# Delta-rule attention and soft MoE on one core: products over two heads on 64-row tiles, a zero-padded state, a 32-column block inverse on VectorE

## The chip, the cores and the metric

The kernel runs on one core of a Trainium2 chip. The metric is device time in microseconds (us) for one launch. The profiled execution is one launch of its own, recorded by the hardware profiler; its time is shown beside the median of the unprofiled runs.

## What is computed

Two blocks follow each other. The first is delta-rule attention over 4 batches, 8 heads, 768 positions and head size 48; the second is a soft mixture of 8 experts with 4 slots each, on rows of 384 numbers.

```
k_n = k / (norm(k) + 1e-06)
for t in range(S):
    y[:, :, t] = q[:, :, t] @ state
    v_old      = k_n[:, :, t] @ state
    state      = state + beta[t] * outer(k_n[t], v[t] - v_old)
x = y with the heads side by side: (3072, 384)
logits = x @ phi                       # 32 slots
d = softmax(logits, over rows);  slot_input = d.T @ x
slot_out[e] = relu(slot_input[e] @ w1[e]) @ w2[e]
out = softmax(logits, over slots) @ slot_out
```

## The kernel before

**Chunks.** The recurrence is done in 24 chunks of C = 32 positions, six groups of GC = 4 chunks. The 32 pairs of batch and head are laid out as four heads `h` on the partitions (32 positions each, slices `hs`) times U = 8 pairs of batch `b` and half `g` in the free dimension. Within a chunk the recurrence becomes matrix products and the inverse of a unit lower triangular 32x32 matrix for each pair.

**Preparation (`prep`).** K and Q of a chunk are loaded by twelve DMAs with V (`loads`, L439), turned by products with the identity (L503), copied to KQ (`copy`: L325 on ScalarE, L327 on VectorE), and multiplied to the Gram matrices K·K and K·Q (L473). The first is copied to Lc, the second multiplied by a triangular mask into AT (L490).

**Inverse (`invert`, once a group).** A 32x32 block transpose puts the four chunks' matrices into lanes (L535). The norms come from the diagonal with two powers on POOL (L541, L544). VectorE inverts the two 16x16 diagonal blocks of each matrix by elimination, 15 pairs of a product and a subtraction (L587, L603), turns them back (L609, L613), POOL or ScalarE mask them (L641, L639), and two sets of products on TensorE give the block below the diagonal (N1, L653, and N2, L666; then L672). The first group does that in four parts, one a chunk; the others in one.

**Chunk loop (`chunk`).** In order: V is scaled by the norms on POOL (L691); R reads the state with K (L704) and the residual is V minus that (L715); W solves with the inverse (L727); evU copies the result; KU adds K times it to the state (L748). Two heads of the state accumulate in two PSUM banks throughout the scan, two are added on VectorE (L760), and both halves are copied to SBUF. Q reads the old state with Q (L704), AU adds AT times U (L771), and evY copies the output, which four DMAs a chunk (`rel`, L783) move to rows of X. Every fourth chunk `route` does the router for 128 positions of each batch (L799, L811, L867). At the end `experts` runs two layers (L1015, L1046) and writes 24 output tiles (L1088).

**What sets the order.** A planner written in the kernel (`Plan`) gives every operation a cost, a priority (the longest path after it, plus a bias) and the buffers it needs (SLOTS, and eight PSUM banks), and simulates the engines. Instructions are then issued to each engine in the order of the planned starts; each engine follows its own order, and waits where an operand isn't there. Expert weights use the scan's buffers as they die; SP issues most loads.

```
SLOTS = dict(K=15, Q=4, V=5, KQ=12, AT=12, Lc=2, lb=1, lbs=1, tt=2, pr=2, Dt=1, Dc=1, M1=1,
...
plan = Plan(SLOTS, 8, 2, 0.15)
...
for o in sorted(plan.ops, key=lambda o: (o.start, o.prio)):
    o.fn(o.eng)
```

Of the kernel before, what the change touches and what calls it, by code (L numbers as in the profile page):

```python
# [35 lines left out]
class Plan:  # L36
# [67 lines left out]
    def run(self, backing=()):  # L104
# [45 lines left out]
        def place(v):  # L150
# [11 lines left out]
            for i in range(0, self.banks - n + 1):  # L162
                if not any(held[i:i + n]):
                    t = max(bank[i:i + n])
                    if best is None or t < best[0]:
                        best = (t, i)
# [77 lines left out]
def kernel(  # L244
# [31 lines left out]
    SIZE = dict(K=U * D, Q=U * D, V=U * D, KQ=B * 2 * P, AT=U * C, Lc=C * C,  # L276
                lb=1056, lbs=512, tt=512, pr=512, Dt=512, Dc=512, M1=512, D0=1024, P1=512,
                TT=C * C, R=U * D, U=U * D, Y=U * D, S=4 * BD, X=B * Dm, XT=B * P,
                lT=P, dT=P, d=P, el=P, cT=P, wt=NKT * F, hr=F, hT=NFC * P, ob=Dm, sj=Dm, so=Dm,
                cw=P, sl=NKT * NSL)  # L280
    SLOTS = dict(K=15, Q=4, V=5, KQ=12, AT=12, Lc=2, lb=1, lbs=1, tt=2, pr=2, Dt=1, Dc=1, M1=1,
                 D0=1, P1=1, TT=2, R=2, U=2, Y=3, S=2, X=2, XT=3, lT=2, dT=1, d=1, el=1, cT=NG,
                 hr=1, hT=2, ob=6, sj=1, so=1, cw=2, sl=1)
    KEEP = ("cT",)
    OBP, HTP, RBIAS, EB = 0, 11, 30.0, 40.0
    TAIL = ("hr", "hT", "ob", "sj", "so", "cw", "sl")
    plan = Plan(SLOTS, 8, 2, 0.15)
    plan.limits = dict(tp=2, pg=2)
# [42 lines left out]

    def vc(n):
        return 0.06 + 0.00104 * n

    hs = [slice(C * h, C * h + C) for h in range(4)]
    rs_ = [slice(DP * g, DP * g + D) for g in range(G)]
# [6 lines left out]
    expo = const("expo", [P, 2])  # L343
# [24 lines left out]
    def constants(e):  # L368
        make_identity(nc, ident)
        PO.memset(expo[:, 0:1], 0.5)  # L370
        PO.memset(expo[:, 1:2], -2.0)
# [15 lines left out]
    op("const2", [("DVE", 1.0)], constants2, [cv], [cv])  # L387

    zv = [val("", "st") for _ in range(2)]

    def zero_banks(e):
        for i in range(8):
            nc.vector.memset(banks[:, i], 0.0)
    op("zero", [("DVE", 3.0)], zero_banks, [], [zv[0]])

    def clear_d0(e):
        for i in range(SLOTS["D0"]):
            PO.memset(where["D0", i].rearrange("p (u s) -> p u s", s=C)[:, :, HC:C], 0.0)
    d0v = val("", "st")
    op("d0", [("POOL", 0.6)], clear_d0, [], [d0v])  # L400
# [9 lines left out]
    def make_sel(e):  # L410
        PO.memset(sel, 0.0)
        for c in range(GC):
            PO.tensor_copy(
                sel[:, c].rearrange("p (h c b g) -> p c h b g", h=4, c=GC, b=B)[:, c],
                ident[0:C, 0:C].rearrange("p (b g h) -> p h b g", b=B, g=G))
# [21 lines left out]
    def load(src, x, cc, h):  # L437
        def fn(e):
            dge[e].dma_start(  # L439
                out=sb(x, U, D)[hs[h]],  # L440
# [11 lines left out]
    KQv, ATv, Lcv = {}, {}, {}  # L452

    def prep(cc):
# [5 lines left out]
        lc = Lcv[n]  # L460
        split = n == 0

        def gram(parts, x):
            def fn(e):
                t = ps(x)
                kt = sb(kq, B, 2, P)
                n0 = len(parts) * C
                for b in range(B):
                    for h in range(4):
                        for g in range(G):  # L470
                            rhs = kt[rs_[g], b, :, hs[h]] if len(parts) == 2 else \
                                kt[rs_[g], b, parts[0], hs[h]]
                            PE.matmul(t[hs[h], g, b * n0:(b + 1) * n0],  # L473
                                      lhsT=kt[rs_[g], b, 0, hs[h]], rhs=rhs,
                                      start=True, stop=True, skip_group_check=True)
            return fn

        def ev_l(x, np_):
            def fn(e):
                src = ps(x)[:, :, 0:B * np_ * C].rearrange("p g (b a t) -> p g b a t", b=B, a=np_)  # L480
                dst = sb(lc, GC, B, G, C)[:, c].rearrange("p b g t -> p g b t")
                copy(e, dst, src[:, :, :, 0, :])
            return fn

        def ev_a(x, np_):
            def fn(e):
                src = ps(x)[:, :, 0:B * np_ * C].rearrange("p g (b a t) -> p g b a t", b=B, a=np_)
                dst = sb(at, G, B, C)
                for g in range(1):
                    nc.vector.tensor_tensor(  # L490
                        dst, src[:, :, :, np_ - 1, :],
                        tri.unsqueeze(1).unsqueeze(1).broadcast_to([P, G, B, C]), op=ALU.mult)
            return fn

        for a, src, L in ((0, Kv, "K"), (1, Qv, "Q")):
# [3 lines left out]
            def tr(e, s=s, tp=tp):  # L499
                t, m = ps(tp, B, P), sb(s, B, G, D)  # L500
                for b in range(B):
                    for g in range(G):
                        PE.matmul(t[rs_[g], b, :], lhsT=m[:, b, g, :], rhs=ident, start=True,  # L503
                                  stop=True, skip_group_check=True)
            op(f"tr{L}{cc}", [("PE", 0.46)], tr, [s, cv], [tp, kq])
# [4 lines left out]
            if split:  # L510
                x = val("pg", "ps", 2)
                op(f"gram{L}{cc}", [("PE", 0.5)], gram((a,), x), [kq], [x, at if a else lc])
                if a == 0:
                    op(f"evL{cc}", [("ACT", 0.4), ("DVE", 0.42)], ev_l(x, 1), [x], [lc], bias=EB)
                else:
                    op(f"evA{cc}", [("DVE", 0.42)], ev_a(x, 1), [x, cv], [at], bias=EB)
        if not split:
            x = val("pg", "ps", 2)
            op(f"gram{cc}", [("PE", 0.58)], gram((0, 1), x), [kq], [x, lc, at])
# [661 lines left out]
```

## Time and profile before

| Figure | Before |
|---|---|
| median of three runs (range) | 518.09 us (515.16 to 520.31) |
| profiled execution, and its span | 509.47 us, 507.8 us |
| mean granted TensorE clock | 0.674 of full |
| first solve (L727) starts | 51.9 us |
| last output product (L771) ends | 444.4 us |
| HBM read and written | 39.47 MB, 4.72 MB |

How to read a profile: times are microseconds, PE is TensorE's matmuls and PEld its weight loads, DVE is VectorE, ACT ScalarE, POOL GpSimd, SP the queue that issues most DMAs. A name such as L704 is a line of the kernel. Rows of the timeline and of the windows give a start or a stretch first, then busy time and, behind an x, the number of instructions; brackets hold the idle time before a row and what ended it. In the windows the last figures are the granted clock, the DMA engines' busy share and GB/s. One call of a product in fp32 shows as two matmul records.

### The profile page before, as it was taken

The page shows a single profiled execution, that of the slowest core. Times are in us where ns is not written, and L with a number is a line of the kernel's source. Part 1 is how long each engine was busy: PE and PEld are TensorE (multiplying, and loading weights), DVE is VectorE, ACT ScalarE, POOL GpSimd, SP SyncE. Part 2 cuts the span into 40 slices and gives each one's busy share as a digit, 9 for nine tenths or more (in the row PEclk, how much of TensorE's full clock was granted, in tenths as well). Part 3 has the DMA queues.
Part 4 walks back from the last instruction along what each step waited for, and adds up shares of the span by engine and source line. Part 5 has one row for each costly group of instructions (what it writes and reads, how often), then busy time and mean ns, then how long its engine had stood idle before and what let it go on. Part 6 is the DMA issues. An engine that isn't in the chain of part 4 may idle for free.

```text
span 507.8 us, 29272 instructions
## 1 busy us (share of the span) xinstructions
PE 344.6 (68%) x13716; PEld 274.9 (54%) x13716; DVE 181.4 (36%) x465; ACT 79.4 (16%) x162; POOL 128.1 (25%) x119
## 2 busy tenths in 40 slices
PE   6737575666776755778567876676755567859974
PEld 5636574555665644666556655455644456533432
DVE  5436225502242512344333453334341122442232
ACT  1114001120121401022300222000220000110022
POOL 4364720050810305400618003180050000000022
PEclk9987559565586955597755885555675555767995
DMA  6643024344014430144111420326534455189837
GB/s 126 122 85 62 5 50 80 59 73 78 4 36 78 74 66 4 30 78 76 21 19 20 70 51 17 102 65 165 158 85 168 137 156 178 20 281 404 327 123 251
DMA packets 115209, 50.81 MB, mean 100 GB/s; under 512 B 105760, under 2 KB 107296, under 8 KB 115088
## 3 DMA queue, kind: packets, MB, share of 16 engines
q1 hardware_dynamic: 89536, 42.05, 32.5%
q10 hardware_dynamic: 24752, 4.48, 5.0%
q8 instruction: 108, 1.77, 1.5%
q0 software_dynamic: 800, 2.41, 1.3%
q14 instruction: 13, 0.11, 0.1%
HBM read 39.47 MB, written 4.72 MB: 87 GB/s over the span
## 4 chain that ended last, share of the span: by engine, by line
PE 50%; issue 32%; DMA 6%; DVE 4%; POOL 3%; SPq 3%; ACT 1%; ACTq 1%; POOLq 0%; DVEq 0%
PE banks L704 8%; PE banks L503 7%; PE banks L771 7%; PE banks L727 6%; PE banks L666 5%; PE banks L748 5%; PE banks L653 5%; PE banks L473 4%; SPq L439 3%; DMA arena<-in_q_dram 2%; PE banks L799 2%; DMA arena<-in_k_dram 1%; DMA arena<-arena 1%; PE banks L867 1%; POOL nrall L541 1%
## 5 line engine op out<-in xcount | busy, mean ns | idle before, releaser
L325 ACT ACTIVATE arena<-banks 128x384 f32<-128x384 f32 (+3 forms) x109 | 55.0, 507 | 372.2 <-PE banks L748 121.4
L327 DVE COPY arena<-banks 128x512 f32<-128x512 f32 (+3 forms) x77 | 43.2, 561 | 133.1 <-PE banks L503 38.5
L503 PE MATMUL banks<-ident,arena 128*48 128x128 f32 x768 | 63.7, 325 | 14.2 <-DMA arena<-in_k_dram 6.1
L704 PE MATMUL banks<-arena 48*32 48x48 f32 x2944 | 48.3, 254 | 30.0 <-issue 29.2
L503 PEld LDWEIGHTS banks<-ident,arena 128*48 128x48 f32 x768 | 53.3, 149 | 20.8 <-issue 13.4
L641 POOL TENSOR_SCALAR arena<-arena,half 128x512 f32<-128x512 f32 (+1 forms) x12 | 19.0, 1597 | 166.5 <-DVE arena L609 78.8
L704 PEld LDWEIGHTS banks<-arena 48*32 48x32 f32 x2944 | 37.9, 130 | 40.7 <-issue 35.3
L771 PE MATMUL banks<-arena 32*32 32x48 f32 x1536 | 35.5, 256 | 16.2 <-issue 16.2
L727 PE MATMUL banks<-arena 32*32 32x48 f32 x1536 | 33.3, 246 | 18.0 <-issue 11.7
L473 PE MATMUL banks<-arena 48*32 48x64 f32 (+1 forms) x1792 | 29.5, 249 | 17.1 <-issue 8.9
L771 PEld LDWEIGHTS banks<-arena 32*32 32x32 f32 x1536 | 29.5, 145 | 20.7 <-issue 19.0
L727 PEld LDWEIGHTS banks<-arena 32*32 32x32 f32 x1536 | 28.1, 138 | 22.5 <-issue 14.5
L653 PE MATMUL banks<-arena 32*32 32x16 f32 x1536 | 24.8, 206 | 19.3 <-issue 18.7
L1088 POOL DMA_DIRECT2D out_dram<-arena x12 | 6.6, 551 | 118.8 <-DVE arena L1084 118.8
L748 PE MATMUL banks<-arena 32*48 32x48 f32 x1472 | 26.4, 266 | 14.1 <-issue 14.1
L666 PE MATMUL banks<-arena 32*32 32x16 f32 x1536 | 26.3, 210 | 13.7 <-issue 13.5
L473 PEld LDWEIGHTS banks<-arena 48*32 48x32 f32 x1792 | 22.8, 122 | 22.5 <-issue 19.9
L653 PEld LDWEIGHTS banks<-arena 32*32 32x32 f32 x1536 | 22.4, 144 | 22.2 <-issue 20.2
L541 POOL TENSOR_TENSOR nrall<-nrall,expo 128x32 f32<-128x32 f32 x6 | 32.7, 5446 | 0.5
L544 POOL TENSOR_TENSOR gmall<-nrall,expo 128x32 f32<-128x32 f32 x6 | 32.7, 5444 | 0.5
L666 PEld LDWEIGHTS banks<-arena 32*32 32x32 f32 x1536 | 24.0, 150 | 16.0 <-issue 15.7
L748 PEld LDWEIGHTS banks<-arena 32*48 32x48 f32 x1472 | 21.4, 160 | 20.0 <-issue 19.0
(110 smaller groups left out, 330.1 us busy)
## 6 DMA issues: line engine op xcount, KB each, us to landing
arena<-in_moe_w_dram SPq DMA_DIRECT2D x24, 512.0 KB, 5.1
arena<-in_moe_w_dram SPq DMA_DIRECT2D x32, 384.0 KB, 7.7
arena<-in_q_dram SPq DMA_DIRECT2D x88, 48.0 KB, 2.5
arena<-in_k_dram SPq DMA_DIRECT2D x87, 48.0 KB, 2.9
arena<-in_v_dram SPq DMA_DIRECT2D x80, 48.0 KB, 2.6
arena<-arena ACTq DMA_DIRECT2D x58, 48.0 KB, 2.3
out_dram<-arena SPq DMA_DIRECT2D x12, 192.0 KB, 2.7
out_dram<-arena POOLq DMA_DIRECT2D x12, 192.0 KB, 3.0
```

Source lines behind the costliest of these rows:

```text
L325: AC.activation(dst, src, ACT.Copy)
L327: nc.vector.tensor_copy(dst, src)
L473: PE.matmul(t[hs[h], g, b * n0:(b + 1) * n0], lhsT=kt[rs_[g], b, 0, hs[h]], rhs=rhs, start=True, stop=True, skip_group_check=True)
L503: PE.matmul(t[rs_[g], b, :], lhsT=m[:, b, g, :], rhs=ident, start=True, stop=True, skip_group_check=True)
L541: PO.tensor_tensor(nrall[:, n], nrall[:, n], expo[:, 0:1].broadcast_to([P, C]), op=ALU.pow)
L544: PO.tensor_tensor(gmall[:, n], nrall[:, n], expo[:, 1:2].broadcast_to([P, C]), op=ALU.pow)
L653: PE.matmul(t[hs[h], u], lhsT=sb(lc, C, C)[hs[h], u], rhs=sb(M1, C, HC)[hs[h], u], start=True, stop=True, skip_group_check=True)
L666: PE.matmul(t[hs[h], u], lhsT=sb(D0, C, C)[hs[h], u], rhs=sb(P1, C, HC)[hs[h], u], start=True, stop=True, skip_group_check=True)
L704: PE.matmul(t[hs[h], g, b * D:(b + 1) * D], lhsT=m[rs_[g], b, a, hs[h]], rhs=s[rs_[g], h, b], start=(b == 0), stop=False, skip_group_check ...
L727: PE.matmul(t[hs[h], u], lhsT=m[hs[h], u], rhs=r[hs[h], u], start=(u == 0), stop=True, skip_group_check=True)
L748: PE.matmul(dst[rs_[g], b * D:(b + 1) * D], lhsT=m[hs[h], b * G + g], rhs=r[hs[h], b * G + g], start=(b == 0 and (h >= 2 or cc == 0)), sto ...
L771: PE.matmul(t[hs[h], g, b * D:(b + 1) * D], lhsT=m[hs[h], g, b], rhs=r[hs[h], b * G + g], start=(cc == 0 and b == 0), stop=True, skip_grou ...
```

## The change

Products in the scan take two heads at a time, or all rows. K and Q lie in SBUF padded from 48 to 64 numbers, so that one transpose turns both halves `g` of a batch. The state keeps `g` as two row blocks of 64 with a zero block beside each (its buffers are cleared once), so that R and Q read it with all 128 rows and 96 columns, and KU writes 128 rows into four PSUM banks that are held through the scan. The Gram product takes two heads on a 64x64 tile; its off-diagonal blocks are masked out, for K·K by two scaled copies on ScalarE and a sum (evL, evM, adL), for K·Q by a copy and a mask on POOL (evA, mkA). The inverse is spread into pairs with zero blocks (`pairs`, TP), for W on 64-row tiles; AU uses the same tiles. `par` and `tri2` are the masks of even and odd heads.

For groups two to six the inverse is an elimination over all 32 columns on VectorE, 31 pairs of steps, without N1 and N2. The norms come from an integer estimate and three Newton steps in place of the powers. Slot counts, biases and the planner's costs of products change too; a product's cost is now at least four times 12.5 ns a call in the plan.

```diff
...
+    SLOTS = dict(K=11, Q=4, V=5, KQ=10, AT=10, Lc=2, Lx=2, lb=2, tt=2, pr=2, Dt=1, Dc=1,
+                 M1=1, D0=1, P1=1, TP=8, R=2, U=2, Y=3, S=2, X=2, XT=3, lT=2, dT=1, d=1, el=1,
+                 cT=NG, hr=1, hT=2, ob=6, sj=1, so=1, cw=2, sl=1)
...
+    OBP, HTP, RBIAS, EB, IBIAS, FETCH = 0, 11, 40.0, 60.0, -5.0, 0.0125
-    plan = Plan(SLOTS, 8, 2, 0.15)
-    plan.limits = dict(tp=2, pg=2)
+    plan = Plan(SLOTS, 8, 0, 0.15)
+    plan.limits = dict(tp=2, pg=2, py=2)
...
+    def pe(mm, array):
+        return [("PE", max(array, FETCH * 4 * mm))]
...
-    rs_ = [slice(DP * g, DP * g + D) for g in range(G)]
+    hp_ = [slice(2 * C * i, 2 * C * i + 2 * C) for i in range(2)]
+    rs_ = [slice(DP * g, DP * g + DP) for g in range(G)]
...
+    for i in range(SLOTS["K"]):
+        for t in ("K", "Q"):
+            if i < SLOTS[t]:
+                padv[t, i] = val("", "st")
+                op(f"pad{t}{i}", [("POOL", 0.3), ("DVE", 0.2)],
+                   lambda e, t=t, i=i: clear(e, where[t, i].rearrange(
+                       "p (u d) -> p u d", d=DP)[:, :, D:DP]), [], [padv[t, i]],
+                   bias=50 - i if i < 4 else 0)
...
+            pad = sb(x).shape[1] // U
             dge[e].dma_start(
-                out=sb(x, U, D)[hs[h]],
+                out=sb(x, U, pad)[hs[h], :, 0:D],
...
+                kt = sb(kq, B, 2, 4, C)
+                m = len(parts) * 2 * C
                 for b in range(B):
-                    for h in range(4):
+                    for hp in range(2):
                         for g in range(G):
...
-                            PE.matmul(t[hs[h], g, b * n0:(b + 1) * n0],
-                                      lhsT=kt[rs_[g], b, 0, hs[h]], rhs=rhs,
-                                      start=True, stop=True, skip_group_check=True)
+                            h2 = slice(2 * hp, 2 * hp + 2)
+                            rhs = kt[rs_[g], b, :, h2].rearrange("p a h t -> p h a t")
...
+                            PE.matmul(t[hp_[hp], g, b * m:(b + 1) * m],
+                                      lhsT=kt[rs_[g], b, 0, h2].rearrange("p h t -> p (h t)"),
+                                      rhs=rhs, start=True, stop=True, skip_group_check=True)
...
-        def ev_l(x, np_):
...
+        def ev_l(x, np_, i, dst):
             def fn(e):
...
+                AC.activation(dst(), view(x, np_, 0)[:, :, :, i], ACT.Copy, scale=par[:, i:i + 1])
             return fn
         def ev_a(x, np_):
             def fn(e):
...
-                    nc.vector.tensor_tensor(
-                        dst, src[:, :, :, np_ - 1, :],
-                        tri.unsqueeze(1).unsqueeze(1).broadcast_to([P, G, B, C]), op=ALU.mult)
+                for g in range(G):
+                    copy(e, sb(at, G, B, 2, C)[:, g], view(x, np_, np_ - 1)[:, g])
             return fn
+        def evs_l(x, np_):
+            dst = lambda: sb(lc, GC, G, B, C)[:, c]
+            op(f"evL{cc}", [("ACT", 0.4)], ev_l(x, np_, 0, dst), [x, cv], [lc, lcp[cc]], bias=EB)
+            op(f"evM{cc}", [("ACT", 0.4)], ev_l(x, np_, 1, lambda: sb(lx, G, B, C)), [x, cv], [lx],
+               bias=EB)
...
+        def evs_a(x, np_):
+            op(f"evA{cc}", pcost2(512), ev_a(x, np_), [x], [at], bias=EB)
+            def mask(e):
+                v_ = nc.vector if e == "DVE" else PO
+                t = sb(at, U, 2, C)
+                v_.tensor_tensor(t, t, tri2.unsqueeze(1).broadcast_to([P, U, 2, C]), op=ALU.mult)
+            op(f"mkA{cc}", [("POOL", 1.15)], mask, [at, cv], [at])
...
-                t, m = ps(tp, B, P), sb(s, B, G, D)
+                t, m = ps(tp, B, P), sb(s, B, G * DP)
                 for b in range(B):
-                    for g in range(G):
-                        PE.matmul(t[rs_[g], b, :], lhsT=m[:, b, g, :], rhs=ident, start=True,
-                                  stop=True, skip_group_check=True)
-            op(f"tr{L}{cc}", [("PE", 0.46)], tr, [s, cv], [tp, kq])
+                    PE.transpose(t[:, b, :], m[:, b, :], ident)
...
+    def pairs(n, c, src, reads, uses):
+        x = TPv[GC * n + c] = val("TP", par=True)
+        for i in range(2):
+            def fn(e, i=i):
+                dst = sb(x, U, 2, C)[:, :, i]
+                if e == "ACT":
+                    AC.activation(dst, src(), ACT.Copy, scale=par[:, i:i + 1])
+                else:
+                    PO.tensor_scalar(dst, src(), par[:, i:i + 1], None, op0=ALU.mult)
+            op(f"TP{GC * n + c}", [("ACT", 0.42), ("POOL", 0.9)], fn, reads + [cv], [x], uses=uses)
...
-        def norms(e):
-            PO.tensor_tensor(nrall[:, n], nrall[:, n], expo[:, 0:1].broadcast_to([P, C]),
-                             op=ALU.pow)
-            PO.tensor_tensor(gmall[:, n], nrall[:, n], expo[:, 1:2].broadcast_to([P, C]),
-                             op=ALU.pow)
-        op(f"norms{n}", [("POOL", 2.0)], norms, [lb, bbv, cv], [gv])
...
+        def newton(e):
+            v_ = nc.vector if e == "DVE" else PO
+            for _ in range(3):
+                v_.tensor_tensor(gm, nr, dg(), op=ALU.mult)
+                v_.tensor_tensor(gm, gm, nr, op=ALU.mult)
+                v_.tensor_scalar(gm, gm, -0.5, 1.5, op0=ALU.mult, op1=ALU.add)
+                v_.tensor_tensor(nr, nr, gm, op=ALU.mult)
+            v_.tensor_tensor(nr, nr, dg(), op=ALU.mult)
+            v_.tensor_scalar(nr, nr, 1e-6, None, op0=ALU.add)
+        op(f"nw{n}", [(E0, 2.6 if n == 0 else 4.5)], newton, [lb, s1], [s1])
...
+        if n:
+            lm = lambda: sb(lb)[:, 0:C * C].rearrange("p (i j) -> p i j", j=C)
...
+            for j in range(C - 1):
+                m, w = j + 1, C - 1 - j
+                pr = val("pr")
+                def e1(e, j=j, m=m, w=w, pr=pr):
+                    t, s, o = sb(tt, C, C), lm(), sb(pr)[:, 0:w * m]
...
+                        nc.vector.tensor_tensor(
+                            o.rearrange("p (i k) -> p i k", i=w),
+                            t[:, j, 0:m].unsqueeze(1).broadcast_to([P, w, m]),
+                            s[:, j + 1:C, j].unsqueeze(2).broadcast_to([P, w, m]), op=ALU.mult)
+                op(f"el{n}.{j}a", [("DVE", vc(w * m))], e1, [tt, lb], [pr])
+                def e2(e, j=j, m=m, w=w, pr=pr):
+                    t, o = sb(tt, C, C), sb(pr)[:, 0:w * m]
+                    d = t[:, 1:C, 0] if m == 1 else t[:, j + 1:C, 0:m]
...
+                    nc.vector.tensor_tensor(d, d, o, op=ALU.subtract)
+                op(f"el{n}.{j}b", [("DVE", vc(w * m))], e2, [tt, pr], [tt])
...
+            return
...
-    keep = val("keep", "st")
+    keep = val("keep", "ps", 4)
...
-        py = val("py", "ps", 2)
+        py = val("py", "ps")
         def read(a, x):
             def fn(e):
-                t, m, s = ps(x), sb(kq, B, 2, P), sb(old, 4, B, D)
+                t, m, s = ps(x, B, G * D), sb(kq, B, 2, P), sb(old, 4, B, G * D)
                 for b in range(B):
                     for h in range(4):
-                        for g in range(G):
-                            PE.matmul(t[hs[h], g, b * D:(b + 1) * D], lhsT=m[rs_[g], b, a, hs[h]],
-                                      rhs=s[rs_[g], h, b], start=(b == 0), stop=False,
-                                      skip_group_check=True)
+                        PE.matmul(t[hs[h], b], lhsT=m[:, b, a, hs[h]], rhs=s[:, h, b],
+                                  start=(b == 0), stop=False, skip_group_check=True)
             return fn
         if cc:
             R = val("R", par=True)
...
         def solve(e):
-            t, m = ps(pw, U, D), sb(T, C, C)[:, c * U:c * U + U]
-            r = sb(R, U, D) if cc else sb(vv, U, D)
-            for u in range(U):
-                for h in range(4):
-                    PE.matmul(t[hs[h], u], lhsT=m[hs[h], u], rhs=r[hs[h], u],
-                              start=(u == 0), stop=True, skip_group_check=True)
-        wo = op(f"W{cc}", [("PE", 0.7)], solve, [TTp[n][c], R] if cc else [TTp[n][c], vv, vs], [pw, Uv],
-           uses=[T])
+            t, m, r = ps(pw, B, G, D), sb(TP, G, B, 2 * C), sb(R if cc else vv, B, G, D)
+            for b in range(B):
+                for g in range(G):
+                    for i in range(2):
+                        PE.matmul(t[hp_[i], b, g], lhsT=m[hp_[i], g, b], rhs=r[hp_[i], b, g],
+                                  start=(b == 0 and g == 0), stop=True, skip_group_check=True)
+        wo = op(f"W{cc}", pe(16, 0.68), solve, [TP, R] if cc else [TP, vv, vs], [pw, Uv])
...
         if cc < NCH - 1:
             new = Sv[cc + 1] = val("S", par=True)
-            ks = val("ks", "ps", 2)
             def update(e):
-                m, r, t = sb(kk, U, D), sb(Uv, U, D), ps(ks)
+                m, r = sb(kk, B, P), sb(Uv, B, G * D)
                 for b in range(B):
-                    for g in range(G):
-                        for h in range(4):
-                            dst = banks[:, h] if h < 2 else t[:, h - 2]
-                            PE.matmul(dst[rs_[g], b * D:(b + 1) * D],
-                                      lhsT=m[hs[h], b * G + g], rhs=r[hs[h], b * G + g],
-                                      start=(b == 0 and (h >= 2 or cc == 0)), stop=True,
-                                      skip_group_check=True)
-            op(f"KU{cc}", [("PE", 0.62)], update, [kk, Uv, zv[0]], [ks, keep])
...
+                    for h in range(4):
+                        PE.matmul(banks[:, h, b * G * D:(b + 1) * G * D], lhsT=m[hs[h], b],
+                                  rhs=r[hs[h], b], start=(cc == 0 and b == 0), stop=True,
+                                  skip_group_check=True)
+            op(f"KU{cc}", pe(16, 0.66), update, [kk, Uv], [keep])
+            for g in range(G):
+                def ev_s(e, g=g):
+                    copy(e, sb(new, 4, B, G, D)[rs_[g], :, :, g],
+                         banks[rs_[g], 0:4, 0:B * G * D].rearrange("p h (b g d) -> p h b g d", b=B,
+                                                                  g=G)[:, :, :, g])
+                op(f"evS{cc}", pcost(768), ev_s, [keep] + s0v, [new], bias=EB)
...
```

## The prediction

> **What bounds the kernel now.** I first read the page's busy shares, then its chain of waits, then its DMA queues, then the timeline of TensorE in the middle, then its windows.
>
> ```profile
> span 507.8 us, 29272 instructions
> PE 344.6 (68%) x13716; PEld 274.9 (54%) x13716; DVE 181.4 (36%) x465; ACT 79.4 (16%) x162; POOL 128.1 (25%) x119
> ...
> q8 instruction: 108, 1.77, 1.5%
> ...
> PE 50%; issue 32%; DMA 6%; DVE 4%; POOL 3%; SPq 3%; ACT 1%; ACTq 1%; POOLq 0%; DVEq 0%
> ```
>
> The chain is TensorE (50%) plus "issue" (32%, 160 us), time in which TensorE waits for nobody. 39 us of it is the expert stage's pipelined matmuls; some 120 us lie in the scan. The timeline, TensorE only, shows what they are:
>
> ```profile
> 200.28 1.47 PE L666 MATMUL banks<-arena 32*32 32x16 f32 x94
> 203.36 0.71 PE L666 MATMUL banks<-arena 32*32 32x16 f32 x34 [1.61 <-issue]
> 204.00 1.37 PE L704 MATMUL banks<-arena 48*32 48x48 f32 x93
> 207.47 0.69 PE L704 MATMUL banks<-arena 48*32 48x48 f32 x35 [2.10 <-issue]
> 208.09 1.50 PE L771 MATMUL banks<-arena 32*32 32x48 f32 x64
> 209.37 0.84 PE L727 MATMUL banks<-arena 32*32 32x48 f32 x29
> 211.20 1.01 PE L727 MATMUL banks<-arena 32*32 32x48 f32 x35 [0.98 <-issue]
> ```
>
> From stop to stop are 34+93 and 35+64+29 matmul records: 128, with their weight loads 256 instructions, wherever a product ends. The page's instruction queue moved 108 packets of 1.77 MB, 16.4 KB each; TensorE's 27,432 instructions over 108 are 254. So TensorE's instruction stream arrives in such blocks and is late. The windows give the rate:
>
> ```profile
> 100.00:150.00 50.00, 32.94 (x1614) 0.61 0.29 49
> 200.00:250.00 50.00, 36.63 (x1645) 0.74 0.30 52
> 300.00:350.00 50.00, 33.52 (x1693) 0.56 0.27 64
> ```
>
> About 1,630 records per 50 us, one block in 3.9 us, at granted clocks from 0.56 to 0.74. So the count of instructions, not array time, sets the scan. The first solve starts at 51.9, the last chunk's output product ends at 444.4: 16.4 us a chunk. A tail of 63 us follows.
>
> **What the Trainium skill says.** "SBUF — State Buffer", section "SBUF: two separate sides": a DVE operation with two SBUF inputs and a GpSimd operation that reads SBUF lock each other out. The trace agrees: two POOL diagonal copies (L560) took 0.34 us alone at 66.67, but 0.86 at 207.68 beside a DVE product of two SBUF inputs (L567, 0.69). "TensorEngine Tiling (Array Packing)", "Key Properties": tiles work in parallel, a change of tiling mode drains. The first shows: 64 records take about 0.95 us on eight tiles (L704), 1.5 on four (L771); a drain's price doesn't. "TensorE: Matmul & The Clock Gate", "What's actually happening": recent activity raises the clock, between half and full. Here the mean is 0.674; the windows agree only in part, since a busier one isn't always faster.
>
> **The change part by part, TensorE.** One call is two matmul records (L704: 1,472 calls, 2,944 records), a true transpose one (L799: 72 and 72). The changed instruction streams hold 3,119 calls, 298 of them transposes: 5,940 records, 46 blocks for 107. At 3.9 us that asks 7.6 us a chunk, no longer a limit if the work itself takes longer.
>
> Busy time after, per record from the nearest row of the groups:
> - K and Q transposes: 192 at 0.199 (L799) = 38 us; before 63.7.
> - State reads, update: 1,472 and 736. With four tiles and 96 columns the nearest is L811 (0.049 for 128 columns): 0.037, so 54.5 and 27.2; before 48.3 and 26.4.
> - Solve, output: 1,536 on two 64-row tiles. L771 is 0.023 on four; between that and twice it I take 0.040: 61, bounds 35 and 71; before 68.8.
> - Gram: 640 at 0.049 and 256 at 0.025 = 38; before 29.4.
> - N1, N2: 512 at 0.0166 = 8.5; before 51.1.
>
> Sum 227 for 288. A chunk needs 9.1 us of it, plus routing (L799, L811, L867 and three small groups, 36 us over 24 chunks = 1.5): 10.6.
>
> **VectorE.** The inverse grows. From the rows of 30 and 126 elements (0.198, 0.289): 0.17 us plus 0.95 ns an element, 0.04 between starts. Before: 30 steps, 2,720 elements, 8.9 us a group. After: 62 steps, 10,912 elements: 10.5+10.4+2.5 = 23.4, in five groups, +72 us. Their transposes in and out (1.9 each), scaling by 1.2 and norms add some 29. In the changed order the fifth inverse ends after the nineteenth residual, so this falls into about 20 chunks. The residuals (0.55), the share of copies from PSUM at 0.42 to 0.69, half of the state copies (768 elements, by slope 0.96) and routing add 48. Together 117+29+48 = 194 us, 9.7 a chunk, with no stall. Zeroing the banks (3.9) goes; the pads take its place at the start.
>
> **ScalarE and POOL.** ScalarE gets two masked copies per Gram (0.38 each), halves of the state (0.8) and 39 pair copies (strided L639 has 0.51 for 128 elements: 0.8 for 256). With 88 DMA issues at 0.65 it has 6.5 us a chunk, covered by TensorE's 10.6; without that cover all of it would count. POOL loses twelve powers, 65 us. It gains 24 masks of 512 elements (L691 has 0.83 for 384: 1.1), 21 sums (0.6), five Newton runs of 14 small operations (about 0.27: 3.8), clears of 1.0 a group: about 4.2 us a chunk. Its waits queue masks behind Newton runs; output products wait for the masks, but those are made many chunks ahead.
>
> POOL and DVE now meet: POOL's 4.2 us a chunk reads SBUF beside inverse steps that take 6 of 9.7. Bounds: nothing if they never overlap, 4.2 if they always exclude. I take 1.5. A gain is excluded, as a lock only delays.
>
> **Queues and PSUM.** SP issues four loads in 2.7 us; about 10.7 loads and 1.7 moves a chunk make 8 us, below 12.9, hence hidden. Slots are fewer (K 11 for 15, KQ 10 for 12), so loads run less far ahead: zero to 1 us a chunk, I take zero, since half the chunks stay as lead. The state now holds four banks, leaving four: each chunk holds pg, tp, pR, pw, py for about 21 bank-us of some 50, so friction, not a limit. Weights keep their place at the end of SP's queue; 24 of the 32 second-layer loads still follow the last move. Tail: 63 us, with bounds 60 and 71.
>
> **The sum.** Start: the norms took 21.3 to 33.5, 12.2 us; sixteen small DVE steps at 0.2 and the reciprocal steps take 4.5. Add 3 for summing the Gram halves, the pair copies and ScalarE's longer queue: first solve at 47 instead of 51.9. Then 20 chunks in which TensorE needs 10.6 and DVE 9.7+1.5 = 11.2, each in a written order and often waiting for the other. I add 15% for that: 12.9 us, 258. Last four chunks: the loop read 1.2, residual 0.55, solve 1.3, copy 0.5, update 1.2, the two state copies 1.7 (the changed order often puts both on one engine: 1.6 on ScalarE, 1.9 on DVE), six hand-overs at some 0.12 = 7.1, with Q and output products in between 9.2: 37. Tail 63. Together 405 us of span against 507.8; 407 as the profiled execution's own 509.47 counts. The median of the three runs before, 518.09, is 1.017 times that execution, so I forecast 414.
>
> **Rivals.**
> - *TensorE alone* bounds, other engines fitting underneath: 10.8 a chunk, tail 61: 47+216+37+61 = 361, by the same steps 369. For it: before the change TensorE hardly waited for others (DVE 4%, ACT 1% of the chain). Against: DVE's load is as large.
> - *Lock and order*: DVE and POOL exclude each other nearly always (9.7+4.2) and 15% is lost: 16 a chunk, tail 65: 47+320+40+65 = 472, by the same steps 482. For it: L560. Against: POOL is idle long enough to be evaded.
> - *The array pays for zeros*: wide tiles at the low clock. L867 shows 0.18 for 384 columns in the scan: 0.045 for 96; with solves at 0.046 TensorE needs 13 a chunk, 15 with friction: 47+300+40+63 = 450, or 459.
> - *Slower*: the long inverse keeps DVE's queue in front of residuals and state copies, so the chunk loop runs at DVE's stalls. It decides from (444-47-37)/20 = 18 us a chunk, 8 above DVE's own work. At 19 the time is 47+380+37+63 = 527, or 538. For it: before, one inverse of 8.9 us stretched from 76.6 to 99.9, because DVE stood in copies that waited for TensorE. Against: those copies came late through the block supply.
> - That the change doesn't cut instructions is excluded by the streams.
>
> **How the numbers follow.** Likeliest 0.57; TensorE alone 0.15; lock 0.13; zeros 0.10; slower 0.05. Range: 372 to 470, from the TensorE case to between the zeros and the lock; it leaves out the slower case, most of the lock and half of the TensorE case. Faster by over 1% 0.93, within 1% 0.02, slower 0.05; 1% is about what a measurement of this kernel tells from no change.
>
> **What would show it.** Right: about 5,940 matmul records, "issue" in the scan below 40 us, DVE near 250 us busy, W-to-W distances of 11 to 14 us, then shorter ones after the last inverse. Wrong: stops every 128 records still there; residuals (now L834) waiting on DVE's own queue; POOL masks of 2 us instead of 1.1; weights landing late in the tail.

## The result, and the profile after

| Figure | After |
|---|---|
| median of four runs (range) | 410.4 us (405.77 to 413.16) |
| before, four runs on the same chip (range) | 517.32 us (515.16 to 520.31) |
| ratio, 95% interval | 0.786 (0.778 to 0.794) |
| profiled execution, and its span | 405.77 us, 404.1 us |
| mean granted TensorE clock | 0.811 of full |
| first solve (L843) starts | 64.4 us |
| last output product (L876) ends | 337.5 us |

The ratio leaves out slow runs (after the change it rests on 405.77 and 407.76 us), so it lies below the quotient of the medians.

The scan gave everything. From the first solve to the last output product it took 273.1 us instead of 392.5, so 119.4 less. The first solve came 12.5 us later, and the tail took 66.6 us instead of 63.4. The three together are the 103.7 us between the two spans.

The page's busy shares, instruction queue and chain of waits after the change:

```profile
span 404.1 us, 14058 instructions
PE 280.0 (69%) x5940; PEld 216.9 (54%) x5940; DVE 277.7 (69%) x633; ACT 131.7 (33%) x277; POOL 119.5 (30%) x198
...
q8 instruction: 47, 0.77, 0.8%
...
issue 7%; DMA 4%; PE 4%; DVE 1%; POOL 1%; ACT 0%; POOLq 0%; DVEq 0%
```

The queue moved 47 packets instead of 108, and TensorE and VectorE are now equally busy. The shares of the chain add up to 17%: it follows the tail and breaks off there, so the scan must be read elsewhere. The windows (busy time and count of TensorE, its weight loads, VectorE, ScalarE and POOL, then granted clock, DMA share, GB/s):

```profile
100.00:150.00 50.00, 34.01 (x855) 28.96 (x851) 39.83 (x86) 17.87 (x35) 17.76 (x28) 0.86 0.40 70
200.00:250.00 50.00, 33.45 (x620) 26.41 (x620) 42.42 (x95) 17.41 (x39) 15.86 (x26) 0.73 0.27 47
```

TensorE works two thirds of these stretches and VectorE 80 to 85%. Neither is full. What TensorE waited for between 64 and 341 us (total, times, longest):

```profile
PE banks L903 <- DMA arena<-arena: 15.5, 3, 8.1
PE banks L843 <- DVE arena L834: 15.0, 15, 2.2
PE banks L1012 <- ACT arena L1000: 5.6, 2, 3.9
PE banks L824 <- ACT arena L327: 4.9, 6, 1.5
...
PE banks L876 <- issue: 1.4, 2, 1.3
```

"Issue" is down to 1.4 us; in the scan before (52 to 444 us) the same list has 110.6 us of it. TensorE's busy time in the scan fell from 266 to 198 us, while its waits for DMA and for other engines grew from 16 to 74 us. The granted clock in these stretches rose from 0.63 to 0.83, so part of the fall in busy time may be the clock's. The largest entry is the routing's transposes (L903), which wait for output rows to be moved. It is paid where one group of chunks follows another. There the timeline of TensorE and SP's queue shows:

```profile
98.15 1.14 PE L843 MATMUL banks<-arena 64*64 64x48 f32 x32
...
111.42 0.59 SPq L887 DMA_DIRECT2D arena<-arena  x1
...
113.50 2.82 PE L903 MATMUL banks<-ident,arena 128*128 128x128 f32 x12 [8.07 <-DMA arena<-arena]
116.25 1.58 PE L915 MATMUL banks<-arena,phi 128*32 128x128 f32 x24
...
119.61 0.61 PE L843 MATMUL banks<-arena 64*64 64x48 f32 x14 [0.46 <-DVE arena L834]
```

The move at 111.42 stood on SP's queue behind twelve loads. TensorE waited 8.07 us for it, with the next solve queued behind. VectorE had a copy of these transposes next in its order, and behind it stood the inverse of the group after. Solve follows solve by 10.0 us on average inside a group (18 distances, 180.0 us), and by 21.5, 19.3, 18.0, 23.2 and 8.1 us across the five changes of group (90.2 us).

The same distances before the change show where the gain lies: the 18 inside groups took 297.7 us (16.5 each), the five changes of group 89.0. So all of it came inside the groups, and the changes of group stayed as long as they were. Before, TensorE waited 27.6 us for instructions at the five changes; now it waits 35 us there for moves, ScalarE and VectorE.

### The profile page after: what moved, and what is told of

It reads as the page before. It is cut to its first block, busy times and chain, and to the rows that moved or that the text cites. A ratio compares the mean times of both kernels' runs of the same rounds, so it can differ in the third digit from the quotient of the medians.

```text
span 404.1 us, 14058 instructions
## 1 busy us (share of the span) xinstructions
PE 280.0 (69%) x5940; PEld 216.9 (54%) x5940; DVE 277.7 (69%) x633; ACT 131.7 (33%) x277; POOL 119.5 (30%) x198
## 5 line engine op out<-in xcount | busy, mean ns | idle before, releaser
L327 ACT ACTIVATE arena<-banks 128x512 f32<-128x512 f32 (+4 forms) x139 | 71.1, 536 | 149.4 <-PE banks L876 36.3
L329 DVE COPY arena<-banks 128x512 f32<-128x512 f32 (+4 forms) x89 | 57.6, 658 | 58.5 <-PE banks L903 18.5
L659 DVE TENSOR_TENSOR arena<-arena 128x31 f32<-128x31 f32 (+15 forms) x155 | 61.7, 398 | 4.1
L648 DVE TENSOR_TENSOR arena<-arena 128x60 f32<-128x60 f32 (+9 forms) x150 | 61.5, 410 | 4.3
L824 PE MATMUL banks<-arena 128*32 128x96 f32 x1472 | 45.2, 271 | 10.3 <-ACT arena L327 4.9
L843 PE MATMUL banks<-arena 64*64 64x48 f32 x768 | 32.8, 244 | 22.8 <-DVE arena L834 15.0
L495 PE MATMUL banks<-arena 64*64 64x128 f32 (+1 forms) x896 | 35.3, 304 | 15.2 <-ACT arena L327 6.4
L843 PEld LDWEIGHTS banks<-arena 64*64 64x64 f32 x768 | 29.9, 159 | 27.7 <-DVE arena L834 14.6
L824 PEld LDWEIGHTS banks<-arena 128*32 128x32 f32 x1472 | 34.7, 120 | 17.9 <-ACT arena L327 10.5
L543 PE MATMUL banks<-ident,arena 128*128 128x128 f32 x192 | 34.1, 328 | 12.2 <-DMA arena<-in_k_dram 10.6
L495 PEld LDWEIGHTS banks<-arena 64*64 64x64 f32 x896 | 28.4, 164 | 20.6 <-ACT arena L327 9.2
L543 PEld LDWEIGHTS banks<-ident,arena 128*128 128x128 f32 x192 | 25.8, 168 | 16.5 <-issue 6.3
L860 PE MATMUL banks<-arena 32*128 32x96 f32 x736 | 30.7, 311 | 5.2 <-DVE arena L329 3.4
L903 PE MATMUL banks<-ident,arena 128*128 128x128 f32 x72 | 16.0, 394 | 26.4 <-DMA arena<-arena 23.6
L533 POOL TENSOR_TENSOR arena<-arena,tri 128x512 f32<-128x512 f32 x24 | 31.9, 1335 | 5.8 <-DVE arena L329 5.0
L876 PE MATMUL banks<-arena 64*64 64x48 f32 x768 | 29.7, 229 | 1.4 <-issue 1.4
L572 ACT ACTIVATE arena<-arena,par 128x256 f32<-128x256 f32 x39 | 25.0, 709 | 16.4 <-DVE arena L663 8.2
```

What stands on the lines that cost most here:

```text
L327: AC.activation(dst, src, ACT.Copy)
L329: nc.vector.tensor_copy(dst, src)
L495: PE.matmul(t[hp_[hp], g, b * m:(b + 1) * m], lhsT=kt[rs_[g], b, 0, h2].rearrange("p h t -> p (h t)"), rhs=rhs, start=True, stop=True, ski ...
L533: v_.tensor_tensor(t, t, tri2.unsqueeze(1).broadcast_to([P, U, 2, C]), op=ALU.mult)
L543: PE.transpose(t[:, b, :], m[:, b, :], ident)
L572: AC.activation(dst, src(), ACT.Copy, scale=par[:, i:i + 1])
```

## The experiments

Ratios are to the kernel before, run on the same chip; the changed kernel has 0.786. A hundredth of the ratio is some 5 us. The order of instructions on every engine is that of the kernel that was edited, unless new planned orders are named.

### Before the change: the solve in two halves

```diff
-PE.matmul(t[hs[h], u], lhsT=m[hs[h], u], rhs=r[hs[h], u], start=(u == 0), ...)
+for z in (slice(0, 24), slice(24, 48)):
+    PE.matmul(t[hs[h], u, z], lhsT=m[hs[h], u], rhs=r[hs[h], u, z], start=(u == 0 and z.start == 0), ...)
```

> The kernel before, with each solve product (L727) issued as two products of 24 columns: 768 matmul records more, the same columns through the array, every engine's order unchanged. Supply theory (TensorE's instructions arrive in blocks of 256, one in 3.9 us): six blocks more, +23 us, about 540. Array theory (the time of the products themselves sets the scan): within 5 us of 517.

Measured: 1.085 (1.074 to 1.096), 554.59 us for 512.42, so 42 us more. The expectation counted calls for records: 768 calls are 1,536 records, twelve blocks, which the supply theory prices at 47 us. The page:

```profile
PE 362.3 (66%) x15252; PEld 291.0 (53%) x15252; DVE 181.5 (33%) x465; ACT 79.4 (14%) x162; POOL 127.7 (23%) x119
...
q8 instruction: 119, 1.95, 1.4%
```

TensorE was busy 18 us longer and the time rose by 42; its waits for "issue" in the scan rose from 110.6 to 138.2 us. Eleven packets more at 3.9 us are 43. Before the change, then, the supply of instructions set the scan.

### After the change: the solve, or the output product, in two halves

The same edit on L843 (solve) and, in a second kernel, on L876 (AU).

> The changed kernel with the same split of its solve products (L843): 768 matmul records more, orders unchanged. VectorE theory (the inverse on VectorE sets the pace of the scan, TensorE has slack): only the solve itself grows, at most some 0.35 us in 24 chunks, 410 to 419. TensorE theory (its instructions still set the pace): six blocks of 3.9 us, about 434.

> The changed kernel (0.786 of the kernel before, some 405 us) with each call of the output product AU in two of 24 columns: 768 more records, 12 more blocks of instructions; all orders stay. Splitting the solve cost 36 us of TensorE and 44 us of time. Chain theory (the loop residual, solve, copy, state update, state copy is what ends last; AU stands beside it): 33 us more of TensorE, but only 5 to 20 us of time, 0.80 to 0.825. TensorE theory (its sum of work, wherever it stands): as the solve, 35 to 45 us, 0.855 to 0.875.

Measured: solve 0.877 (0.866 to 0.888), AU 0.855 (0.849 to 0.861): some 47 and 36 us more for 768 records each. VectorE's theory (no change) and, for AU, the chain theory's 0.825 fall. But the 434 us of TensorE's theory for the solve were too low as well: 768 records are six blocks (53 packets for 47; the second expectation has twelve), which would be 23 us, and the stops didn't come back ("issue" took 1.6 and 2.4 us of the scan). What grew is TensorE's busy time, from 280.0 us to 341.9 and 324.9, at a granted clock of 0.731 and 0.757 for 0.811. The groups of the solve's kernel, the split solve (L844) and the unsplit AU (L878), with busy time and mean ns of one:

```profile
L844 PE MATMUL banks<-arena 64*64 64x24 f32 x1536 | 68.8, 247 | 24.3 <-DVE arena L834 16.8 <-POOL arena L574 2.4 <-ACT arena L572 2.2
L878 PE MATMUL banks<-arena 64*64 64x48 f32 x768 | 35.9, 257 | 1.6 <-issue 1.6
```

With half the columns a record takes nearly as long here: 45 ns busy for 24 columns, 47 for 48 in the same profile. In the kernel with AU split it is 38 ns for AU's 24 columns and 49 for the solve's 48. The distances between solves say where the time went. Inside groups they grew from 10.0 to 12.0 us for the solve, which lies in the state loop, and to 11.0 for AU, which doesn't. The changes of group grew from 90 to 101 and 103 us. So more TensorE work costs time wherever it stands, and about twice as much inside groups when it is in the loop.

### Less work on VectorE

Two kernels: POOL's mask of K·Q (L533) turned into two clears that read nothing, so that POOL doesn't lock VectorE there (AT is then zero, and the output products multiply zeros); and the elimination's steps on one column instead of up to 31.

```diff
-v_.tensor_tensor(t, t, tri2.unsqueeze(1).broadcast_to([P, U, 2, C]), op=ALU.mult)
+v_.memset(sb(at), 0.0)
+v_.memset(sb(at), 0.0)
```
```diff
+nc.vector.tensor_tensor(o[:, 0:w], t[:, j, 0:1].broadcast_to([P, w]), s[:, j + 1:C, j], op=ALU.mult)
...
+d = t[:, j + 1:C, 0]
+nc.vector.tensor_tensor(d, d, o[:, 0:w], op=ALU.subtract)
```

> The changed kernel with each POOL mask of AT (L533, reads two operands) replaced by two clears of AT (no reads, about 1.06 us for 1.33), orders unchanged; the output products are left out in effect. Lock theory (POOL's reads block VectorE's steps with two SBUF operands): the inverse's instructions shorten towards 0.34 us on the mean from 0.40, the first solve comes some 5 us earlier than 64.4, and the whole falls by 15 to 30 us, to 380 to 396. Order theory (VectorE loses its time in its written order, not to POOL): within 5 us of 410.

> The changed kernel whose elimination steps in groups two to six work on one column only, 31 pairs of instructions as before in the same order, some 47 us of VectorE less (9,920 elements a group fewer at 0.95 ns, five groups); most of the inverse is left out. VectorE theory: the scan shortens until TensorE's 10 to 10.6 us a chunk bound it, 360 to 385. TensorE theory: above 400.

Measured: clears 0.785 (0.774 to 0.796), small steps 0.768 (0.760 to 0.777). VectorE's busy time fell from 277.7 us to 259.6 and 227.8, and the time by nothing and by some 9 us (give or take 6, from the two intervals). The 394 us of the small steps lie between the ranges of both theories. The lock of this mask costs VectorE 18 us, and its absence gave the kernel nothing. One thing moved against it, though: with the clears TensorE was busy 9 us longer (289.0 us), at a granted clock of 0.777. In the other kernel 50 us of VectorE were worth a fifth of themselves. VectorE's load isn't the bound.

### Less work on TensorE, and on both

```diff
-for i in range(2):
+for i in range(2 if b == 0 else 0):    # AU
```

> The changed kernel with the output product AU for the first batch only (three quarters of AU are left out), orders unchanged: 576 records and some 22 us of TensorE less; AU isn't in the state loop. TensorE theory (its work costs time wherever it stands, as 33 us more did): 15 to 22 us less, 0.74 to 0.757 of before. Loop or VectorE theory (there is slack beside AU, and the split runs only used it up): 0 to 6 us less, 0.772 to 0.787.

> Both engines relieved at once, orders unchanged: AU for the first batch only (three quarters of AU left out, 576 records less) and the elimination steps of groups two to six on one column only (the inverse left out in effect, VectorE some 50 us less). Alone they gave 0.803 and 0.768, the changed kernel 0.786. Interlock theory (TensorE and VectorE each hide what the other is spared): more than both together, 0.70 to 0.745. Order theory (the hand-overs of the written order, the moves and loads by DMA and the changes of group set the pace, and neither engine's load does): nothing is added, 0.76 to 0.79.

Measured: AU for one batch 0.803 (0.796 to 0.811), some 9 us slower than the changed kernel, which neither theory had; with the small steps 0.763 (0.760 to 0.766), about as the small steps alone. The ranges of TensorE's theory and of the interlock theory were not met. But that doesn't refute either of them, because 576 records less didn't relieve TensorE. Two pages, the changed kernel's being above:

```profile
PE 286.5 (70%) x5364; PEld 218.6 (53%) x5364; DVE 277.8 (68%) x633; ACT 131.9 (32%) x277; POOL 118.9 (29%) x198
```

```profile
PE 276.5 (71%) x5364; PEld 212.3 (54%) x5364; DVE 227.8 (58%) x633; ACT 131.6 (34%) x277; POOL 116.8 (30%) x198
```

The first has a granted clock of 0.736 for 0.811, the second 0.756 for 0.820 of the small steps alone. The records that stayed became slower: the state reads took 51.2 us for 45.2. What was taken out came back as slower records. So no run here shows what less TensorE time would give.

### Routing later

The plan gets one more dependency: the transposes of a group's rows wait for the second solve of the next group. The planner makes new orders from it; routing stands in them behind the first one or two chunks of the next group.

```diff
 op(f"xt{n}.{kt}", [("PE", 0.46)], tr, [X, cv], [tp, xt[kt]],
+   after=[solves[GC * n + GC + 1]] if n < NG - 1 else [])
```

> The changed kernel with the routing of a group planned behind the second solve of the next group, not ahead of its first (the plan gives new orders; the work is the same). Boundary theory: at each change of group TensorE stands at the routing's transposes until the last output rows have been moved (8.1 us at 113.5), with the next group's first chunk queued behind it; a change of group costs 10 to 12 us more than a chunk within a group. Then the solves 98 to 119 us come closer by 5 or more, and the time is 375 to 395 us (0.73 to 0.765 of before). VectorE theory (its own work sets the pace): 400 to 408 us, as the changed kernel (0.775 to 0.79).

> Both: the routing behind the second solve of the next group, and the elimination steps of groups two to six on one column only (the inverse is left out in effect). Small steps alone gave 0.768 for 0.786. If VectorE's load was hidden behind the waits at the change of group, it shows now: 345 to 370 us (0.67 to 0.715), more than the two gains added. If the two gains only add, 365 to 385 us. If neither was on the path, 390 and above.

Measured: 410.16 us for 515.62 (quotient 0.795; its runs spread from 400 to 422 us, so no interval), and 0.782 (0.777 to 0.786) with the small steps. No gain; together slower than the small steps alone. The first change of group fell from 21.5 to 15.6 us, as the boundary theory says, but the second took 21.1. VectorE, ScalarE, POOL and TensorE at that second change:

```profile
163.52 1.25 DVE L663 STREAM_TRANSPOSE arena<-arena 128x1024 f32<-128x1024 f32 x1
164.80 2.64 ACT L572 ACTIVATE arena<-arena,par 128x256 f32<-128x256 f32 x4 [8.07 <-DVE arena L663]
164.86 1.18 POOL L574 TENSOR_SCALAR arena<-arena,par 128x256 f32<-128x256 f32 x1 [0.54 <-DVE arena L663]
...
166.10 1.20 PE L845 MATMUL banks<-arena 64*64 64x48 f32 x18 [9.53 <-POOL arena L574]
```

The inverse of that group ended only at 164.8, because its steps are spread over VectorE's order up to there, and its pairs released the solve. The order counts here more than the length of the steps: with the small steps this change still took 20.2 us, and the solve waited 7.5 us for the same pairs. In the changed kernel that inverse ended at 160.5 us and the solve started at 164.3. So an inverse nearly as late stood behind the wait for moved rows.

### The start

The second group's inverse planned behind the first group's last step.

```diff
-op(f"spread{n}", [("DVE", 1.6)], spread, [lc], [lb])
+op(f"spread{n}", [("DVE", 1.6)], spread, [lc], [lb], after=first if n == 1 else [])   # first: the ops TTb
```

> The changed kernel with the second group's inverse planned behind the last step of the first group's (TTb). Start theory: the first solve was late (64.4 us) because VectorE turned and began the second group's inverse ahead of the first group's last steps and waited there for POOL's Newton steps: first solve at 57 to 61 us, time 3 to 8 us less (0.77 to 0.78). Rival: the second group's inverse then ends later and its first solve with it, so that nothing is left of it by the fifth solve: 0.78 to 0.79.

Measured: 0.837 (0.833 to 0.842), 26 us slower. The first solve came at 70.1 us, not earlier: in the new order all four TTb stand behind the four copies of N1's results, and wait there for N2. The changes of group took 107 us for 90. Both sides missed; it shows only how much a changed order can cost, with TensorE's and VectorE's busy time little changed (289 us for 280, and 282 for 278).

### Two parts of the change undone

W and AU on 32-row tiles, reading the diagonal blocks of the paired matrices:

```diff
-for i in range(2):
-    PE.matmul(t[hp_[i], b, g], lhsT=m[hp_[i], g, b], rhs=r[hp_[i], b, g], ...)
+for h in range(4):
+    o = slice(C * (h % 2), C * (h % 2) + C)
+    PE.matmul(t[hs[h], b, g], lhsT=m[hs[h], g, b, o], rhs=r[hs[h], b, g], ...)
```

> The changed kernel with one part undone: W and AU on 32-row tiles again, reading the diagonal blocks of the paired matrices; 1,536 more records (7,476), the same results and the same orders. Array theory (what counts is the time of TensorE's array; before the change these products took 68.8 us on 32-row tiles, after it 62.5 on 64-row tiles): 3 to 12 us more, 0.79 to 0.81 of before. Supply theory (records count; twelve blocks of 128 at 3.9 us): 40 to 50 us more, 0.865 to 0.885, as in both split runs. VectorE theory: no change, 0.78 to 0.79.

Measured: 0.819 (0.812 to 0.826), some 17 us more, between the array's 12 and the supply's 40. The records are 7,476 and the packets 59, yet TensorE was busy 283.8 us for 280.0. A record on four 32-row tiles takes 18.7 ns for 42.7 on two 64-row tiles. In the profiled execution, 12 us longer, the scan took 10.2 us more and the tail 4.7, with a first solve 2.6 us earlier. What TensorE waited for shows the scan's part (60 to 350 us):

```profile
PE banks L844 <- issue: 4.2, 4, 2.8
...
PE banks L824 <- issue: 3.6, 2, 2.7
...
PE banks L878 <- issue: 2.3, 4, 1.0
```

With two smaller entries "issue" makes 11.6 us in 12 stops, for 1.4 us in the changed kernel, and the stops lie 126 to 128 records, or a multiple of some 127, apart. So the stops of the kernel before came back in part, and they are as large as what the scan lost.

The inverse of all groups in two 16x16 blocks, with N1 and N2 on TensorE, and new planned orders:

```diff
-    if n:
+    if False:
-SLOTS = dict(K=11, Q=4, V=5, KQ=10, AT=10, Lc=2, Lx=2, lb=2, tt=2, ...)
+SLOTS = dict(K=11, Q=4, V=5, KQ=9, AT=10, Lc=2, Lx=1, lb=1, tt=1, ...)
-ALIAS = {("X", 1): [("D0", 0), ("Dt", 0)], ("XT", 0): [("Dc", 0)], ...}
+ALIAS = {}
```

> The changed kernel with another part undone: the inverse of all six groups by two 16x16 eliminations and N1, N2 on TensorE, as the first group has it. 2,560 more records of about 17 ns (42 us of TensorE), some 80 us less of VectorE. To fit, one KQ, one Lx, one lb, one tt buffer fewer, none shared with the router. TensorE theory: slower than the changed kernel by 20 to 45 us, 0.825 to 0.875 of before, although VectorE loses a quarter of its work. VectorE theory: 20 to 40 us faster, 0.71 to 0.75.

Measured: 0.849 (0.840 to 0.858), some 32 us slower than the changed kernel, although VectorE loses 40 us of work (277.7 to 237.6; its elimination steps fell from 139 to 59 us, but copies, N1's among them, came to it). In the profiled execution, 34 us longer, solves inside groups keep 9.9 us; the changes of group take 114.6 us for 90.2, and the tail 76.9 for 66.6, which wasn't followed up. What TensorE waited for from 60 to 360 us:

```profile
PE banks L771 <- issue: 11.4, 4, 5.6
PE banks L771 <- ACT arena L757: 11.2, 3, 7.2
PE banks L842 <- DVE arena L833: 9.8, 5, 4.7
PE banks L784 <- issue: 8.6, 5, 2.1
```

N1 (L771) waits for its masked operands and for instructions, N2 (L784) for instructions, and the solve stands behind both. Of the waits for instructions 20.7 us fall between the first solve and the last output product, 15.1 of them at the changes of group. The smaller buffers of this kernel are in the 32 us too; what they cost alone wasn't tried.

## Why the prediction held, and where it didn't

**The bound before** was named rightly; the halved solve confirms the block and its price (43 us worked out from packets, 42 measured). After the change the stops every 128 records are gone, as forecast, with 5,940 records, 47 packets and 1.4 us of "issue" in the scan (below 40 forecast).

**The total** was right (414 forecast, 410.4 measured), but two terms of the sum were off by 17 and 18 us, in opposite directions. That they cancel is luck. The profiled execution against them:

| Term | Forecast | Measured |
|---|---|---|
| first solve | 47 | 64.4 |
| 20 chunks | 258 (12.9 each) | 239.8 (12.0 each) |
| last four chunks | 37 | 33.3 |
| tail | 63 | 66.6 |
| sum | 405 | 404.1 |

**The start** was mis-sized by 17 us. The step took 7.7 us off the norms and added 3 for sums and copies. It left out what stands around VectorE's small steps there: copies, the second group's spread, and POOL's masks and scaled V's, which meet them. The timeline of VectorE and POOL:

```profile
37.96 1.27 POOL L533 TENSOR_TENSOR arena<-arena,tri 128x512 f32<-128x512 f32 x1
38.09 1.20 DVE L704 TENSOR_TENSOR arena<-arena 128x56 f32<-128x56 f32 x1
...
54.04 0.18 DVE L704 TENSOR_TENSOR arena<-arena 128x56 f32<-128x56 f32 x1
...
61.04 0.30 POOL L609 TENSOR_SCALAR nrall<-nrall 128x32 f32<-128x32 f32 x1
61.38 0.35 DVE L613 RECIPROCAL gmall<-nrall 128x32 f32<-128x32 f32 x1 [2.55 <-POOL nrall L609]
62.10 0.28 DVE L791 TENSOR_TENSOR arena<-arena,banks 128x128 f32<-128x128 f32 x1
```

One product of 56 elements took 1.20 us beside the mask and 0.18 without it. The spread began at 24.8 us (19.3 before), the Newton steps took 7.4 us instead of 4.5, the first inverse 18 instead of 9.9, with three copies and the second group's spread between its steps. At the end it waited 2.55 us for POOL's Newton steps of the second group, ahead of the first group's last step (L791). Taking the mask's lock away brought the first solve to 62.5 only, so this lock explains 2 of the 17 us; the rest lies in the late spread and in the order, or in locks that stayed.

**TensorE's rows** held in the sum and not one by one: solve and AU 62.5 us (forecast 61), transposes 34.1 (38), Gram 35.3 (38), state reads 45.2 (54.5), update 30.7 (27.2), N1 and N2 7.6 (8.5). They add to 215 for 227. The clock, 0.811 for 0.674, wasn't in the forecast.

**VectorE** was busy 277.7 us for 250. The inverse's steps took 127 us where 104.5 were forecast. The lock's allowance of 1.5 us a chunk (30 us in all) fits so far: 18 us came back when only the K·Q mask's lock was removed, and the other locks weren't measured. The masks took 1.335 us for 1.1. Removing that lock gave the kernel nothing.

**The scan's step failed in its mechanism.** The forecast took the larger of two loads a chunk, VectorE's, and added 15% everywhere. The runs show that VectorE's load doesn't set the pace: 50 us less of it gave 9. TensorE's load stays open: no run made it clearly smaller (275.8 us was the least), and 62 and 45 us more of it cost some 47 and 36. It isn't the bound by itself, since TensorE worked 198 of the scan's 273 us.

The friction isn't even either. A chunk inside a group takes 10.0 us on average (6.6 to 16.4), near the 9.2 forecast for the last chunks, and a change of group 18, four of the five 18 to 23. Only three of the 23 distances lie in the 11 to 14 us that were forecast; the mean of 12 mixes the two kinds. At the changes, routing, the last steps of an inverse and the first chunk of a group stand in one written order. Faster chunks and those changes gave together what the 15% had stood for.

**The rivals.** *Lock and order* forecast 482 us, and taking the mask's lock away moved nothing. *Slower* needed VectorE's queue to hold residuals up; solves waited 15.0 us in all for residuals. *TensorE alone* needed the other engines to fit underneath, at 369 us; they didn't: in the scan TensorE waited 31 us for VectorE, 22 for ScalarE and 18 for DMA. *Zeros*: paired tiles cost 62.5 us against 55.8 for single ones, so the pairs with their zeros cost 7 us of TensorE, yet single ones were slower for the kernel.

**Where the gain came from.** Undone in the changed kernel, two parts have a price: pairs of heads in W and AU some 17 us, the 32-column inverse some 32, if the smaller buffers of that kernel cost little. In both, the stops for instructions came back in the scan (11.6 and 20.7 us), so part of what these changes are worth is still fewer records. The remaining half (whole transposes, the state's 64-row blocks, the wider Gram) wasn't taken apart. It stays open, too, whether an order exists in which the changes of group cost no more than a chunk: both orders tried moved the wait instead of removing it, and no complete version was shown to beat the changed kernel.

## What to carry to other kernels

When a bound by instruction supply is lifted and two engines come out equally busy, don't forecast with the larger load and a percentage: measure a step of the loop, and look for the places where work of another period (here a group of four chunks) cuts into every engine's order. A wait that is removed there uncovers the one beside it, so name the second before promising the first. And before reading a run in which work was left out, look at the busy time of the engine that should have been relieved: here three quarters of a product were gone, and TensorE was busy as long as ever.

## What the runs showed of the hardware

On two 64-row tiles a record took 45 ns for 24 columns and 47 for 48 in one profile, 38 and 49 in another; on four 32-row tiles 48 columns took 18.7 ns. More tiles at work shortened a record more than fewer columns did. The Trainium skill, "TensorEngine Tiling (Array Packing)", "Key Properties", says that tiles work in parallel, and 18.7 ns on four tiles for 42.7 on two agrees.

A block of 128 records in 3.9 us makes 30 ns a record, an estimate from the windows before the change. The changed kernel's reads, solves, updates and output products take 31 to 43 ns, and it waited 1.4 us for instructions. In the two kernels with parts undone, where many records of 15 to 19 ns (N1, N2, or the products on 32-row tiles) follow each other, the stops were back.

Twice, taking AU records out left TensorE's busy time about as it was (280.0 to 286.5, 275.8 to 276.5 us), with a lower granted clock (0.811 to 0.736, 0.820 to 0.756). The Trainium skill, "TensorE: Matmul & The Clock Gate", "What's actually happening", says that the clock follows recent activity. Whether records count as that activity these runs don't show: the split kernels, with more records, had 0.731 and 0.757, and the clears, with the same records as the changed kernel, 0.777. A test of the clock by itself wasn't made.
